# A fused RWKV-5 and SwiGLU kernel: first chunk loaded by halves, one table on another engine, merged stores, branch hints and a new order of all operations

## Chip, cores and metric

The kernel runs on one core of a Trainium2 chip. The metric is the device time of one execution in microseconds (us). Each time given as a median comes from several executions; a profiled execution is one more, taken with the hardware profiler, whose span runs from the first to the last instruction.

## What is computed

Two blocks follow each other. The first is a linear attention with a decaying state: for each of 4 batches and 8 heads, a 48 x 48 state runs over 768 time steps. The second takes its output as 3072 tokens of 384 features, normalises each by its root mean square and applies a gated feed-forward layer with 1536 hidden features.

```python
for t in range(S):                                   # S = 768, D = 48
    cur = einsum('bhd,bhe->bhde', u * k[t], v[t])
    y[t] = einsum('bhd,bhde->bhe', r[t], state + cur)
    state = w * state + einsum('bhd,bhe->bhde', k[t], v[t])
x = y.transpose(0, 2, 1, 3).reshape(B * S, H * D)    # (3072, 384)
xn = x / sqrt(mean(x * x) + 1e-6) * rms_g
g = xn @ w_gate
out = (g * sigmoid(g) * (xn @ w_val)) @ w_out
```

All inputs are float32; the weights arrive as float64 and are cut to 32 bits on the chip.

## The kernel before

**Tiling.** The 768 steps are cut into 12 chunks of 64 (`NS`, `L`). For a chunk, the attention is turned into matrix products: scores of r against k with powers of w folded in, masked, times v; plus r against the state. With 4 batches a chunk gives 256 tokens for the feed-forward layer. The 8 heads lie as 2 x 4 on the two halves of 64 partitions. Chunks 0 and 1 go through the layer as plain products while the weights still arrive; from chunk 2 on, chunks go in pairs, with a scheme that needs seven products for eight.

**Mixing of chunk 0** (`mixing`, L807, with `quick`). It works on two halves of the batches, q = 0 and 1, so that one half can go ahead. `CH` holds r and k of a chunk, channels on partitions. ScalarE makes ku = k times u (`u_k`, L466), four products a half. VectorE makes `RR` = r times the table `up`; VectorE (half 0) and GpSimd (half 1) make k times the table `down` in place (`decay`, L440). TensorE makes the products E of ku and r and A of k and RR (`products`, L482), 32 matmuls a half. VectorE takes the diagonal from E and the rest from A into the masked scores `MT`. TensorE makes the outputs Y = `MT` times `V` (`first_outputs`, L516). ScalarE then keeps them (yT), their squares (sq) and a copy with the partition halves exchanged (yb, L629). The squares give the norm: TensorE sums them, GpSimd takes a power, VectorE refines it and puts it on a diagonal (diag), a matmul spreads it to all rows (spread) and ScalarE copies it. Chunk 0's first hidden products start before the norm is there, and take it in afterwards.

**Tables.** `powers` (L327) raises w to the powers 0 to 63 on VectorE into `pw`. `up` is `pw` over w to the 32nd, made by `table_up` (L339) with eight ScalarE products of 64 columns; `down` is the mirror image, one VectorE product of 512 columns.

**Weights.** SP loads them in pieces of 384 or 576 numbers a partition (`piece`, L395) into six raw buffers. ScalarE (ulp) and VectorE (two operations on bits) cut each piece, and GpSimd adds the two parts. At most four loads are in flight (`IN_FLIGHT`): the fifth is issued when the first has landed (`at_most`, L164).

**Order.** Every operation is first added to a plan with an engine, a cost and the keys that it reads and writes. `Plan.give` (L230) then issues all operations in the order of the list `ORDER` (L83), written out as numbers: each engine runs its own operations in that order. Waits follow from data alone. Before the first useful matmul, `warm` (L1095) issues some matmuls of 512 columns on a tile of ones, as many as the planned start of that matmul leaves room for.

**End.** The fast path holds for a range of inputs only. It counts violations into `bad`; behind the last matmul each engine loads that number (`load`, L1289), and `program` (L1698) branches over a general version of some 5,000 instructions when it is zero. In the program text the general version comes directly behind the fast one, so with zero every engine jumps. The last results leave by `result` (L1171): with 64 rows to a DMA, the two halves of the rows go out on SP and ScalarE, and the very last piece by two DMAs on ScalarE.

**Stores of chunks 0 and 1.** `store` (L674) issues a DMA for each 64 rows, four a chunk.

Of the kernel before, what the change touches and what calls it, by code (L numbers as in the profile page):

```python
# [61 lines left out]
HP = H // 2  # L62
# [10 lines left out]
def feature_order():  # L73
# [10 lines left out]
    0, 4, 5, 14, 9, 6, 1, 39, 19, 3, 8, 2, 16, 17, 24, 11, 44, 12, 40, 41, 29, 43, 45, 10, 42, 47, 74, 99, 46, 49, 50,  # L84
    20, 13, 56, 48, 15, 51, 96, 57, 18, 34, 25, 7, 52, 58, 26, 27, 53, 21, 60, 22, 63, 59, 31, 109, 64, 23, 54, 65,
    55, 81, 66, 104, 61, 62, 28, 67, 114, 30, 82, 68, 119, 32, 69, 122, 70, 75, 101, 33, 83, 76, 86, 102, 100, 87, 36,
    77, 120, 106, 78, 35, 71, 121, 98, 80, 123, 97, 79, 37, 130, 124, 107, 196, 73, 191, 125, 38, 91, 105, 201, 127,
    72, 103, 126, 92, 129, 128, 108, 115, 88, 131, 110, 116, 145, 132, 151, 117, 188, 133, 111, 152, 112, 193, 270,
    153, 113, 93, 134, 135, 187, 275, 136, 118, 206, 197, 190, 137, 155, 138, 156, 194, 139, 159, 157, 192, 140, 198,
    280, 141, 199, 160, 142, 195, 285, 154, 161, 148, 200, 144, 162, 189, 163, 143, 203, 146, 214, 164, 147, 211, 171,  # L90
    165, 158, 89, 94, 212, 172, 213, 167, 173, 202, 150, 174, 168, 208, 237, 183, 169, 204, 271, 170, 223, 302, 205,
    184, 166, 179, 185, 209, 207, 215, 276, 307, 180, 268, 186, 210, 175, 149, 181, 218, 272, 176, 224, 277, 278, 217,
    251, 182, 177, 282, 220, 273, 216, 274, 221, 219, 247, 84, 222, 252, 178, 95, 248, 253, 281, 254, 348, 243, 249,
    286, 283, 225, 90, 322, 279, 250, 267, 312, 317, 226, 349, 244, 238, 229, 259, 287, 245, 85, 227, 263, 246, 304,
    230, 260, 303, 228, 305, 288, 261, 231, 284, 262, 327, 232, 255, 350, 332, 289, 264, 233, 256, 306, 265, 257, 240,
    351, 357, 269, 294, 266, 319, 314, 295, 309, 374, 298, 296, 239, 258, 297, 299, 313, 315, 290, 300, 358, 301, 310,
    291, 308, 234, 318, 337, 387, 311, 241, 408, 292, 361, 391, 360, 352, 323, 392, 316, 293, 236, 242, 354, 388, 320,
    321, 389, 353, 355, 359, 407, 342, 356, 329, 324, 334, 330, 390, 362, 325, 561, 326, 363, 399, 333, 335, 235, 565,
    338, 564, 328, 400, 364, 366, 367, 393, 331, 365, 573, 562, 368, 339, 343, 369, 563, 340, 336, 370, 571, 341, 344,
    394, 570, 371, 381, 410, 372, 375, 384, 345, 376, 382, 383, 405, 346, 377, 373, 378, 409, 439, 347, 568, 587, 395,  # L100
    440, 379, 594, 574, 406, 396, 567, 397, 566, 572, 401, 418, 398, 593, 411, 385, 569, 402, 620, 412, 413, 414, 403,
    575, 621, 404, 622, 576, 441, 577, 447, 442, 579, 444, 448, 588, 449, 415, 443, 445, 589, 630, 450, 446, 580, 380,
    453, 451, 452, 454, 581, 458, 624, 455, 457, 460, 459, 582, 462, 461, 623, 463, 456, 632, 590, 464, 629, 465, 595,
    466, 592, 591, 469, 467, 419, 468, 416, 646, 472, 417, 470, 421, 477, 473, 471, 578, 653, 583, 479, 478, 474, 420,
    386, 625, 424, 652, 485, 476, 480, 481, 486, 631, 627, 487, 482, 475, 626, 633, 496, 483, 484, 488, 797, 491, 489,
    584, 497, 498, 422, 492, 628, 493, 504, 423, 495, 499, 427, 500, 505, 425, 506, 798, 490, 501, 585, 494, 502, 634,
    503, 635, 800, 507, 510, 508, 509, 515, 511, 513, 512, 517, 516, 514, 638, 426, 523, 639, 430, 518, 519, 524, 636,
    525, 799, 520, 428, 534, 647, 521, 522, 648, 526, 801, 804, 529, 527, 535, 530, 640, 536, 531, 810, 533, 528, 542,
    537, 586, 532, 539, 429, 543, 433, 431, 538, 540, 641, 545, 541, 544, 553, 548, 554, 432, 649, 546, 549, 809, 436,
    599, 637, 651, 550, 547, 650, 555, 551, 600, 552, 596, 601, 802, 806, 603, 556, 434, 597, 558, 598, 437, 607, 435,  # L110
    606, 438, 807, 604, 803, 605, 602, 608, 829, 642, 654, 557, 805, 611, 560, 823, 559, 830, 643, 655, 644, 610, 645,
    609, 612, 808, 656, 613, 811, 615, 614, 860, 616, 812, 617, 856, 813, 815, 816, 659, 817, 618, 683, 657, 619, 658,
    685, 684, 824, 691, 686, 857, 662, 688, 692, 818, 693, 687, 689, 694, 690, 858, 825, 697, 695, 702, 698, 859, 699,
    704, 703, 696, 701, 710, 660, 705, 661, 700, 707, 711, 665, 663, 814, 868, 708, 826, 706, 713, 709, 712, 716, 714,
    721, 717, 718, 720, 723, 722, 715, 729, 664, 724, 719, 666, 726, 730, 667, 725, 727, 869, 671, 668, 862, 731, 732,
    728, 866, 882, 735, 733, 740, 736, 737, 739, 742, 741, 734, 748, 865, 743, 738, 863, 745, 749, 744, 746, 751, 747,
    669, 750, 754, 752, 753, 759, 755, 670, 756, 674, 761, 760, 758, 831, 889, 763, 762, 757, 764, 827, 767, 765, 766,
    770, 768, 769, 773, 771, 772, 778, 774, 828, 775, 672, 780, 819, 779, 675, 861, 673, 777, 781, 888, 786, 676, 677,
    867, 680, 776, 783, 787, 788, 782, 784, 789, 785, 864, 792, 790, 791, 793, 870, 795, 794, 796, 832, 835, 820, 834,
    872, 836, 838, 871, 873, 681, 874, 837, 875, 678, 833, 679, 876, 1036, 839, 877, 1033, 878, 682, 843, 879, 821,  # L120
    1034, 840, 881, 822, 880, 846, 844, 883, 1035, 842, 1039, 1043, 1037, 1042, 847, 891, 884, 845, 1040, 892, 848,
    885, 849, 1059, 921, 850, 851, 919, 894, 852, 887, 920, 853, 886, 893, 895, 922, 841, 854, 1038, 855, 924, 927,
    925, 1041, 923, 928, 898, 1044, 1066, 890, 930, 926, 929, 933, 931, 938, 934, 935, 937, 940, 939, 896, 897, 946,
    941, 1045, 901, 943, 947, 932, 948, 936, 942, 899, 944, 1046, 957, 945, 900, 949, 904, 952, 950, 1092, 958, 959,
    951, 953, 954, 965, 956, 960, 902, 1047, 1093, 903, 955, 907, 1065, 1048, 962, 966, 961, 963, 1060, 967, 1049,
    968, 964, 971, 969, 1051, 976, 1094, 972, 978, 977, 973, 970, 975, 984, 979, 905, 1052, 980, 985, 1098, 986, 974,
    981, 1101, 995, 982, 983, 987, 990, 988, 996, 997, 991, 992, 906, 994, 1053, 998, 999, 989, 910, 1054, 993, 1000,
    1003, 1001, 1002, 1006, 1004, 1095, 908, 1061, 1009, 1005, 1096, 909, 1014, 1102, 1010, 1007, 1011, 1062, 1015,
    1067, 1118, 1018, 1099, 1013, 1125, 911, 1016, 1064, 913, 912, 1022, 1017, 1008, 916, 1105, 1063, 1019, 1023,
    1104, 1012, 1020, 1097, 1021, 1124, 1025, 1100, 1050, 1103, 1028, 1026, 1027, 1029, 1106, 1024, 1030, 1031, 1032,  # L130
    1071, 1068, 914, 1055, 917, 915, 1072, 1069, 1074, 918, 1056, 1070, 1058, 1107, 1079, 1269, 1073, 1108, 1075,
    1080, 1110, 1111, 1272, 1273, 1112, 1076, 1078, 1083, 1113, 1077, 1109, 1270, 1271, 1119, 1114, 1082, 1084, 1115,
    1116, 1085, 1120, 1121, 1081, 1117, 1087, 1155, 1127, 1088, 1156, 1089, 1123, 1057, 1122, 1282, 1128, 1281, 1295,
    1276, 1129, 1302, 1279, 1274, 1090, 1157, 1130, 1091, 1126, 1086, 1163, 1158, 1160, 1164, 1278, 1165, 1159, 1161,
    1275, 1166, 1162, 1174, 1167, 1131, 1134, 1168, 1169, 1175, 1176, 1170, 1171, 1173, 1182, 1177, 1277, 1178, 1183,
    1184, 1172, 1179, 1193, 1180, 1181, 1185, 1280, 1188, 1186, 1328, 1187, 1283, 1194, 1189, 1190, 1132, 1192, 1195,
    1133, 1285, 1137, 1201, 1196, 1191, 1198, 1202, 1135, 1203, 1296, 1197, 1199, 1136, 1212, 1200, 1297, 1140, 1329,
    1301, 1284, 1204, 1207, 1205, 1213, 1214, 1208, 1206, 1209, 1211, 1220, 1138, 1215, 1330, 1216, 1221, 1139, 1222,
    1210, 1217, 1335, 1143, 1334, 1231, 1218, 1287, 1141, 1223, 1142, 1288, 1219, 1146, 1224, 1289, 1226, 1332, 1225,
    1232, 1233, 1227, 1331, 1228, 1239, 1230, 1234, 1235, 1240, 1341, 1229, 1290, 1236, 1241, 1250, 1237, 1238, 1242,  # L140
# [40 lines left out]
class Plan:  # L181
# [30 lines left out]
    def times(self, order, free):  # L212
# [3 lines left out]
        for i in order:  # L216
# [9 lines left out]
            if locks:  # L226
                port[e] = end[i]
        return start

    def give(self, order, free, idle, final):  # L230

        assert sorted(order) == list(range(len(self.ops)))
        start, busy = self.times(order, free), 0.0
        last = next(i for i in reversed(order) if self.ops[i][0] == "PE")
        for i in order:
# [4 lines left out]
            if i == last:  # L240
                final()
# [1541 lines left out]
```

## Time and profile before

| | us |
|---|---|
| median of 3 executions | 603.48 |
| lowest, highest | 599.68, 604.60 |
| the profiled execution | 599.91 |
| its span, first to last instruction | 598.2 |

| engine | busy us of the span | share |
|---|---|---|
| TensorE matmul (PE) | 583.4 | 98% |
| TensorE weight load (PEld) | 512.6 | 86% |
| VectorE (DVE) | 411.2 | 69% |
| ScalarE (ACT) | 296.2 | 50% |
| GpSimd (POOL) | 46.2 | 8% |

How to read the profile: almost all lines carry L178, since one helper issues every operation; groups are told apart by the tiles, written out<-in. Waits are put down to the semaphore that came last. The page cuts the span into 40 slices and gives each engine's busy share in tenths, so that a hole in an engine's work can be placed; the DMA row does the same for the 16 DMA engines. Times of branches and semaphore instructions are shown but not counted as busy. A matmul's end is modelled, so a busy PE does not mean that it runs at its peak.

### The profile page before, as it was taken

To read this page: it belongs to the slowest core of one execution; us is meant where nothing else is said; L and a number is where in the kernel's file an instruction comes from. 1 tells how busy PE (TensorE), PEld (TensorE's weight loads), DVE (VectorE), ACT (ScalarE), POOL (GpSimd) and SP (SyncE) were. 2 spreads that over 40 slices of the span, in tenths; PEclk is the share of its full clock that TensorE was granted. 3 is DMA by queue.
4 is the path that set the end of the run, shared out by engine and by line. 5 is a ranking of instruction groups with operands and counts; after the bars stand their busy time and mean duration, and the time that the engine had idled before them with its cause. 6 is when DMAs were issued, how large, how long until landed. Compare 5 with 4: busy or idle time off the path is not lost.

```text
span 598.2 us, 16446 instructions
## 1 busy us (share of the span) xinstructions
PE 583.4 (98%) x7202; PEld 512.6 (86%) x7202; DVE 411.2 (69%) x621; ACT 296.2 (50%) x721; POOL 46.2 (8%) x40
## 2 busy tenths in 40 slices
PE   7889999999999999999999999999999999999995
PEld 4678888667888899888899888899888899988995
DVE  7857786877887786666877566878558775455631
ACT  6755666663656633662383356627355652113300
POOL 3342323600000000000000000000000000000000
PEclk8989999999999999999999999999999999999999
DMA  8786384125251233213302530501523200201001
GB/s 283 262 280 256 133 291 141 53 69 173 67 201 32 62 119 116 65 54 115 125 8 67 168 113 28 211 10 35 169 65 115 95 9 1 80 28 54 2 22 38
DMA packets 22546, 62.99 MB, mean 105 GB/s; under 512 B 2977, under 2 KB 9793, under 8 KB 21057
## 3 DMA queue, kind: packets, MB, share of 16 engines
q1 hardware_dynamic: 21760, 61.41, 30.5%
q8 instruction: 58, 0.95, 0.7%
q10 hardware_dynamic: 704, 0.44, 0.3%
q14 instruction: 24, 0.19, 0.1%
HBM read 56.04 MB, written 4.72 MB: 102 GB/s over the span
## 4 chain that ended last, share of the span: by engine, by line
PE 94%; DVE 2%; ACT 1%; issue 1%; DMA 1%; POOL 0%; SPq 0%; DVEq 0%; ACTq 0%
PE bank_b L178 32%; PE bank_a L178 26%; PE bank_c L178 26%; PE at L178 10%; DMA chan<-in_chan_dram 1%; DVE RR L178 1%; DVE bits L178 0%; ACT ku L178 0%; DVE MT L178 0%; ACT up L178 0%; DVE ms L178 0%; ACT ST L178 0%; DVE KH L178 0%; POOL ms L178 0%; SPq L178 0%
## 5 line engine op out<-in xcount | busy, mean ns | idle before, releaser
L178 DVE TENSOR_TENSOR gv<-bank_b,m 128x512 f32<-128x512 f32 x90 | 62.1, 690 | 60.6 <-PE bank_b L178 59.0
L178 ACT ACTIVATE gv<-gv 128x512 f32<-128x512 f32 (+1 forms) x60 | 31.2, 524 | 72.5 <-DVE gv L178 71.8
L178 DVE TENSOR_TENSOR gv<-bank_c,gv 128x512 f32<-128x512 f32 x60 | 41.5, 691 | 23.6 <-PE bank_c L178 23.2
L178 PE MATMUL bank_b<-xa,wa 64*128 64x256 f32 x444 | 55.8, 385 | 0.0
L178 PEld LDWEIGHTS bank_b<-xa,wa 64*128 64x128 f32 x444 | 43.4, 191 | 5.6 <-issue 0.3
L178 PE MATMUL bank_a<-xa,wa 64*128 64x256 f32 x372 | 45.6, 378 | 0.0
L178 PE MATMUL bank_a<-xb,wb 64*128 64x256 f32 x372 | 45.6, 378 | 0.0
L178 PE MATMUL bank_a<-wo,h 128*128 128x192 f32 x264 | 45.6, 329 | 0.0
L178 PE MATMUL bank_b<-t,s 64*128 64x256 f32 x360 | 44.5, 379 | 0.0
L178 PE MATMUL bank_c<-t,s 64*128 64x256 f32 x360 | 44.2, 378 | 0.0
L178 PE MATMUL bank_b<-t,wb 64*128 64x256 f32 x360 | 44.1, 377 | 0.0
L178 PE MATMUL bank_c<-xb,s 64*128 64x256 f32 x360 | 44.0, 377 | 0.0
L178 PEld LDWEIGHTS bank_a<-wo,h 128*128 128x128 f32 x264 | 42.9, 190 | 0.5
L178 ACT COPY m<-bank_a 128x512 f32<-128x512 f32 (+1 forms) x35 | 19.9, 570 | 46.9 <-PE bank_a L178 31.7
L178 ACT ACTIVATE MT<-dmask,du 128x64 f32<-128x64 f32 x160 | 41.3, 339 | 1.3 <-DVE du L178 1.2
L178 PEld LDWEIGHTS bank_a<-xb,wb 64*128 64x128 f32 x372 | 35.8, 187 | 4.6 <-issue 0.6
L178 PEld LDWEIGHTS bank_a<-xa,wa 64*128 64x128 f32 x372 | 35.8, 187 | 4.6 <-issue 0.6
L178 ACT ACTIVATE rows_out<-rows_out 128x384 f32<-128x384 f32 x72 | 39.2, 558 | 0.4
L178 DVE TENSOR_TENSOR h<-gv 128x256 f32<-128x256 f32 (+1 forms) x60 | 32.6, 551 | 9.2 <-ACT gv L178 9.0
L178 PEld LDWEIGHTS bank_c<-xb,s 64*128 64x128 f32 x360 | 34.8, 187 | 4.3 <-issue 0.3
L178 PEld LDWEIGHTS bank_c<-t,s 64*128 64x128 f32 x360 | 34.6, 187 | 4.3 <-DVE h L178 0.3
L178 PEld LDWEIGHTS bank_b<-t,wb 64*128 64x128 f32 x360 | 34.7, 187 | 4.0
(179 smaller groups left out, 1074.5 us busy)
## 6 DMA issues: line engine op xcount, KB each, us to landing
chan<-in_chan_dram SPq DMA_DIRECT2D x11, 1024.0 KB, 6.9
TOK<-in_tok_dram SPq DMA_DIRECT2D x10, 768.0 KB, 5.5
V<-in_vpad_dram SPq DMA_DIRECT2D x12, 512.0 KB, 4.6
raw<-in_wot_dram SPq DMA_DIRECT2D x8, 576.0 KB, 4.3
rows_out<-in_wka_dram SPq DMA_DIRECT2D x12, 384.0 KB, 3.3
rows_out<-in_wkb_dram SPq DMA_DIRECT2D x12, 384.0 KB, 3.3
rows_out<-in_wot_dram SPq DMA_DIRECT2D x12, 384.0 KB, 3.2
out_dram<-rows_out SPq DMA_DIRECT2D x41, 96.0 KB, 2.8
```

The source lines that it names most:

```text
L178: return lambda *args, **kwargs: self.tc.keep_in_program_order(give(*args, **kwargs))
```

## The change

The change has six parts.

- `loads(0)` issues r and k of chunk 0 as four DMAs, one for each half of the batches, instead of two. A half has 2 KB a partition.
- `table_up` is one VectorE product of 512 columns, with the factors repeated by the access pattern.
- `store` sends the results of a chunk with two DMAs, each with two batches of 64 rows, instead of four.
- `result` sends the last piece by one DMA on SP and one on ScalarE.
- Ahead of the fourth matmul group from the end, each engine gets a branch hint for the branch over the general version, behind its last instruction issued by then; the branch is marked to prefer falling through.
- `ORDER` is another permutation. The formula for the number of warm-up matmuls has other constants; three are issued instead of four.

In the new order SP's queue begins: the small columns, r half 0, k half 0, k half 1, r half 1, one weight piece, V, four weight pieces, r and k of chunk 1, k by tokens of chunk 1, six large or small weight pieces, V of chunk 1. Before, it began: the columns, k, two weight pieces, r, a weight piece, V, two weight pieces, a large one, r and k of chunk 1, a weight piece, k by tokens, three large pieces, V of chunk 1.

```diff
 ORDER = [
-    0, 4, 5, 14, 9, 6, 1, 39, 19, 3, 8, 2, 16, 17, 24, 11, 44, 12, 40, 41, 29, 43, 45, 10, 42, 47, 74, 99, 46, 49, 50,
+    0, 4, 7, 5, 6, 8, 1, 11, 41, 10, 2, 16, 3, 42, 43, 21, 45, 26, 12, 46, 44, 76, 47, 49, 31, 48, 51, 52, 17, 13, 53,
...
-    def give(self, order, free, idle, final):
+    def give(self, order, free, idle, hint, final):
...
-        last = next(i for i in reversed(order) if self.ops[i][0] == "PE")
+        last = [i for i in order if self.ops[i][0] == "PE"][-4:]
         for i in order:
+            if i == last[0]:
+                hint()
...
-            if i == last:
+            if i == last[-1]:
                 final()
...
     def table_up():
-        for x in range(2 * HP):
-            act.mul(flat3(up)[:, x], pw[:, x], winv[:, x : x + 1])
+        dve.tensor_mul(flat3(up), pw, by_inv)
...
-    def store(osb, s, j):
+    def store(sums, s):
         for bl in range(2):
-            row = (2 * j + bl) * S + s * L
-            sp.dma_start(out=out[row : row + L, :], in_=osb[bl * L : (bl + 1) * L, :])
+            to = bass.AP(
+                tensor=out.tensor, offset=out.offset + (bl * S + s * L) * DM, ap=[[DM, L], [2 * S * DM, 2], [1, DM]]
+            )
+            sp.dma_start(out=to, in_=sums[bl * L : (bl + 1) * L])
...
             for i, x in ((1, "k"), (0, "r")):
-                add(
-                    "SP", 1.5, [], [f"CH{x}0", f"CH{x}1"],
-                    lambda i=i: sp.at_most(IN_FLIGHT, lambda: sp.dma_start(out=CH[:, i], in_=chan[s, :, i])), land=LAND, name=f"load {x} {s}",
-                )
+                for q in range(2):
+                    half = slice(2 * q, 2 * q + 2)
+                    add(
+                        "SP", 0.75, [], [f"CH{x}{q}"],
+                        lambda i=i, half=half: sp.at_most(
+                            IN_FLIGHT, lambda: sp.dma_start(out=CH[:, i, half], in_=chan[s, :, i, half])
+                        ), land=LAND, name=f"load {x} {s}",
+                    )
...
-    add("ACT", 2.0, ["pw", "h3.1", "h3.2"], ["up"], table_up, name="up")
+    add("DVE", 0.65, ["pw", "h3.1", "h3.2"], ["up"], table_up, port=True, name="up")
...
-            for _ in range(int((until - 4.5) / 0.9)):
+            for _ in range(int((until + 0.4 - 3.75) / 0.86)):
...
-            if last and k == 1 and js == (1,):
-                add("ACT", 1.0, keys, [f"stored {s} {k} {js}'"], lambda: give((0, 1), act), land=2.5, name="store")
-            elif last:
+            if last:
                 add("SP", 0.6, keys, [f"stored {s} {k} {js}"], lambda: give((0,), sp), land=2.5, name="store")
                 add("ACT", 0.6, keys, [f"stored {s} {k} {js}'"], lambda: give((1,), act), land=2.5, name="store")
...
+    def hint():
+        traced = nc.cur_bb.bb.instructions
+        for engine in mybir.ALL_ENGINES:
+            with tc.issue_after(next(i for i in reversed(traced) if i.engine == engine)):
+                tc.mark_branch_hint_location("general", "LikelyTaken", [engine])
...
-    with tc.If(n_bad > 0):
+    with tc.If(n_bad > 0, preferred_fallthrough_block=True, label="general"):
```

## The prediction

> **What bounds the kernel now.** I read first the busy time by stage, since a mean over the span hides where TensorE idles. Columns: stretch in us, its length, then busy us of PE, weight loads, VectorE, ScalarE and GpSimd, granted clock, DMA share, GB/s.
>
> ```profile
> core 0: us, PE busy (x) PEld busy (x) DVE busy (x) ACT busy (x) POOL busy (x), PEclk, DMA share, GB/s
> 0.00:9.50 9.50, 6.23 (x8) 2.37 (x8) 5.43 (x24) 5.58 (x18) 1.42 (x11) 1.00 0.77 259
> 9.50:18.00 8.50, 7.40 (x237) 6.78 (x237) 6.97 (x16) 5.92 (x18) 4.91 (x4) 0.80 0.87 305
> ...
> 38.00:591.50 553.50, 553.50 (x6563) 490.30 (x6560) 380.06 (x550) 271.05 (x657) 30.94 (x19) 1.00 0.28 94
> 591.50:598.20 6.70, 0.01 (x1) 0.00 (x0) 0.36 (x1) 0.00 (x0) 0.00 (x0) 0.89 0.12 33
> ```
>
> From 38 us to 591.5 us PE never pauses, and the change takes no matmul from it. So time can be won only in the first 38 us and in the last 6.7 us, and lost anywhere. The 6.23 us of PE work before 9.5 us are 8 warm-up passes that compute nothing. Next the chain of waits for the head: start, us, what.
>
> ```profile
> 1.25 4.06 DMA chan<-in_chan_dram
> ...
> 5.40 1.28 ACT ku L178 x4
> 6.68 1.91 ACT up L178 x8
> 8.59 0.89 ACT ku L178 x3
> ...
> 9.52 2.37 DVE RR L178 x2
> ...
> 14.28 1.05 PE bank_c L178 x32
> 15.34 0.86 issue
> ...
> 35.10 1.73 issue
> ```
>
> k of chunk 0 lands at 5.31; ScalarE then makes half of ku, all of up, then the other half of ku, and VectorE's RR starts at 9.52, because r, issued fourth, lands at 9.42. The two pieces "issue" are stalls for which the profile names no data. Last the instructions of the branch line, for the tail:
>
> ```profile
> L1704 PEldq COMPARE_BRANCH  x1: 3912/3912/3912, 589.0 to 589.0; - x1
> L1704 SPq COMPARE_BRANCH  x1: 45/45/45, 590.5 to 590.5; - x1
> L1704 ACTq COMPARE_BRANCH  x1: 54/54/54, 593.3 to 593.3; - x1
> L1704 ACTq EVENT_SEMAPHORE  x1: 17/17/17, 597.0 to 597.0; - x1
> ```
>
> ScalarE branches at 593.3 and its next instruction runs at 597.0: 3.7 us for a jump. SP branches at 590.5 and runs on at 594.0: 3.5 us.
>
> [...]the two RR products took 0.69 and 1.76 us, the second beside GpSimd's 1.49. [...]four in flight share some 350 GB/s, and 512 KB took 4.06 us.
>
> **The change, part by part.**
>
> *Loads.* Before, SP issues k, two weight pieces, r. After: r half 0, k half 0, k half 1, r half 1, then one weight piece, V. That is two issues more (2 x 0.43 us on SP, hidden: SP waits for landings anyway). Behind them the first weight piece is issued when the first half lands instead of at 1.7 us; VectorE takes it later (below). The second half to be issued completes 512 KB, as k alone did, so I take 5.3 for k half 0; 5.9 and 6.4 for the next two at 350 GB/s. Bounds: [...]6.3 (before, the second transfer landed at 6.25).
>
> *Table up.* Removed: 8 ScalarE products, 2.0 us. Added: one VectorE product, 0.69 us by the row of its twin "down", which took 4.70 to 5.39. VectorE is idle 0.88 us there, waiting for weights; cover enough. It ends at 5.4, down at 6.1.
>
> *The head, step by step.* ScalarE: ku 5.4 to 6.65 and 6.65 to 7.95 (1.28 each). VectorE: RR half 0 6.1 to 6.8, k half 0 to 7.5, RR half 1 to 8.2 (0.69 each). GpSimd: k half 1 8.0 to 9.5 (1.49). PE: scores E at 6.7 and 8.0, A half 0 to 9.2 (0.57 for 32 matmuls, half of the 1.15 at half clock). VectorE: mask 9.3 to 10.05 (0.77). PE: outputs half 0 10.1 to 11.0 (0.9), where before they ran 13.30 to 14.2: 3.2 us earlier. VectorE now puts one weight piece (0.36 + 0.56) between the halves, so its last mask ends at 12.45 against 14.56: 2.1 earlier. But ScalarE, which comes next, is loaded first by half 0: yT 0.89, squares 0.5, a copy 0.5, a weight piece 0.55, squares, yT, three copies: 11.1 to 16.5, against 20.05 before. 3.5 earlier. The norm, then the spread matmul, start at 18.1, against 21.69.
>
> *What is late next.* Chunk 1's r and k (1 MB) can only be issued when A half 1 has read chunk 0's: 11.6 against 13.31. Before it took 6.87 us, so 18.5; by bytes alone 16.3. ScalarE's order puts ku of chunk 1 (1.28) and a weight piece (0.55) ahead of the copy of the norm, so that copy comes at 18.7 to 20.4, against 22.42. So 2.0 to 3.7 us of the lead survive. The weights do not eat it: in the trace wa and wb of the second quarter are ready at 32.15 and 33.52 and used at 37.98 and 40.56.
>
> *The clock and the two stalls.* With three warm-up rows for four (4.7 us of work for 6.23) [...]one window at half clock may fall on the outputs of chunk 0: 0.9 + 0.57 us more, at worst 1.5 lost. The 0.86 stall may vanish, as the stretch before it is now spread out: between 0 and 0.86 won. The 1.73 at 35.1 sits in a run of 64-row products that the new order keeps as dense: I take no change, 0 to 1.73 won[...]. I take 3.0 us for the whole head, 0.5 to 6.
>
> *The order after 38 us.* PE changes its kind of product (full, halves, quarters) 93 times instead of 90; a change costs 0.1 to 0.2 us (groups of 1.50 against 1.29 hold one or two). 0.3 us lost. Whether new waits arise the trace can't show; bounds 0 and, by the rival below, some us.
>
> *Merged stores of chunks 0 and 1.* Two SP issues for four, twice: 4 x 0.33 to 0.4 us off a queue that nobody waits for then; the landings hide behind PE. Nothing.
>
> *Tail.* The last result was stored by two ScalarE DMAs one after the other, 591.94 and 592.45, the second 0.81 us long and 3.9 us to landing: 596.3. From there to the end 1.85 us (SP's row of waits, two barriers). After: one on SP, one on ScalarE, both at 592.0. The stores around took 1.9 to 4.1 us to landing, median 2.7; I take 2.1[...]: 594.1, and the end at 595.95. 2.2 us won. That needs the hint: without it SP jumps at 592.45 + 3.5 and the end is at 597.9: 0.3 won. The hint is not in the trace[...]. The five hint instructions themselves should cost no more than the branch, 45 ns. I take the hint as working; the general path still lies first in the program, so the jump remains.
>
> Sum: 3.0 - 0.3 + 2.2 = 4.9 us. The profiled execution took 599.91 (span 598.2 and 1.7 around it); after: 595.0. It lies 3.6 us below the median of the runs shown, 603.48; the same difference there gives 598.6.
>
> **Rivals.** (1) *More*: [...]4.9 + 0.86 + 1.73 + 1.0 = 8.5 us, 595.0. For it: both stalls lie where DMA is 0.87 and 0.77 busy; against: the same instructions, as dense. (2) *The hint does nothing*: 4.9 - 1.9 = 3.0, 600.5. For it: no row shows one. (3) *The head wins nothing*, because four halves share the DMA engines and land together at 8 us (before, the third transfer landed at 8.15): tail alone, 601.5. (4) *Slower: V of chunk 1.* On SP it stands behind six weight pieces that follow the 1 MB load and the small token load (before, four), 8.85 MB into the stream instead of 8.26. Its outputs stood at 33.57 on PE, with no other work before them. By 13.5 us 3.54 MB had landed; at 350 GB/s from there V lands at 28.7, in time; the point is 38.6, 5 us after the old place (head lead and tail gain used up), a stream of 211 GB/s from 13.5 us on. Before it ran 253 at 20 to 30 us. Each us beyond is a us lost; a DMA queue that waits for raw buffers could bring 44.8: 603.48 + 6.2 = 609.7.
>
> **How the numbers follow.** 1% (6.03 us) is about what a measurement of this kernel can tell from no change. Forecast 0.57: 598.6, own range 596.5 to 600.5; a quarter of it is over 1% faster. Rival 1: 0.19, faster. Rival 2: 0.11 and rival 3: 0.05, within 1%. Rival 4: 0.08, nearly all slower. Faster 0.14 + 0.19 = 0.33; slower 0.07; the same 0.60. The range 594.5 to 604.5 leaves out half of rival 4 and the ends of rival 1 and of the forecast's.
>
> **What would show it.** In the profile after: k half 0 landing by 5.9, RR starting near 6.1, outputs of chunk 0 near 10, the spread near 18 to 20, PE without a pause from 36 on; in the tail under 0.6 us between each branch and the next instruction, and the last store's landing about 2 us after its issue. I am wrong if PE shows gaps after 38 us, if the branch still costs 3.5 us, or if the outputs of chunk 1 start after 32.

## The result, and the profile after

The changed kernel takes 599.02 us (median of 20 runs, 596.73 to 602.77) where the kernel before, run beside it, takes 599.98 (20 runs): a ratio of 0.9992 with a 95% interval of 0.9968 to 1.0015. No change that this measurement can tell from none. The prediction said 4.9 us less; by the ratio about 0.5 came (0.96 between the medians), and the interval reaches from 1.9 us less to 0.9 more. The profiled execution took 598.84 us, span 597.1, against 599.91 and 598.2 before. The rest of the document looks for the missing 4 us.

First the busy time by stage of the changed kernel, with the stretches of the table shown of before. Columns: stretch, length, then busy us of PE, weight loads, VectorE, ScalarE and GpSimd, granted clock (the share of its full clock that TensorE was given), DMA share, GB/s.

```profile
core 0: us, PE busy (x) PEld busy (x) DVE busy (x) ACT busy (x) POOL busy (x), PEclk, DMA share, GB/s
9.50:18.00 8.50, 6.87 (x140) 6.33 (x140) 4.53 (x13) 5.67 (x16) 2.31 (x3) 0.58 0.92 322
18.00:23.40 5.40, 4.99 (x27) 3.60 (x26) 4.48 (x10) 2.95 (x9) 2.87 (x3) 0.72 0.95 342
23.40:38.00 14.60, 12.06 (x359) 9.88 (x363) 13.71 (x21) 9.57 (x20) 5.79 (x5) 1.00 0.80 277
38.00:591.30 553.30, 553.09 (x6589) 489.61 (x6577) 388.69 (x554) 270.80 (x657) 29.04 (x19) 1.00 0.29 94
```

From 38 us on TensorE pauses for 0.21 us in all, in one new wait at 107.5 us. What is new is the clock: 0.58 in 9.5 to 18 us where before it was 0.80, and 0.72 in the next stretch. The clock records show half clock from 10.83 to 21.07 us, 10.24 us in a row; before, it lay at 9.69 to 13.10 and at 36.99 to 40.41, 3.41 and 3.42 us long. So a window means here a stretch of 3.41 us at half clock: the changed kernel has three in a row. Now the chain of waits of the head: start, us, what.

```profile
6.28 1.22 PE bank_c L178 x32
...
9.29 0.77 DVE MT L178 x2
...
10.36 1.20 PE at L178 x48
...
15.43 2.65 PE at L178 x12
18.08 4.28 PE bank_a L178 x24
22.36 0.64 PE at L178 x2
...
23.03 0.37 ACT diag L178
...
36.31 1.32 issue
37.63 0.77 PE at L178 x37
```

The front works as planned: E starts at 6.28, and the outputs of chunk 0 ("at", x48) at 10.36, where they started at 13.30. But the copy of the norm ("ACT diag") comes at 23.03, where before it came at 22.42. A lead of 2.9 us has become a lag of 0.6, and the chain names TensorE itself for it: mean squares 2.65 us, the first 24 weight products 4.28. The products are not alone in their place. While TensorE made them, the norm went its own way over GpSimd and VectorE, and its diagonal was ready (22.23) just when TensorE was free to spread it (22.29):

```profile
21.75 0.48 DVE L178 TENSOR_SCALAR diag<-ident,ms 128x128 f32<-128x128 f32 x2
...
22.29 0.70 PE L178 MATMUL at<-diag,ones 128*128 128x256 f32 x2
```

In the other runs of the new head without fillers the spread came 0.35 to 1.2 us behind the diagonal, so there the products at half clock did hold it up. Last the branch line, for the tail.

```profile
L1715 PEldq COMPARE_BRANCH  x1: 398/398/398, 589.2 to 589.2; - x1
L1715 DVEq COMPARE_BRANCH  x1: 84/84/84, 591.4 to 591.4; - x1
L1715 SPq COMPARE_BRANCH  x1: 70/70/70, 592.3 to 592.3; - x1
L1715 ACTq COMPARE_BRANCH  x1: 73/73/73, 593.2 to 593.2; - x1
L1715 DVEq EVENT_SEMAPHORE  x1: 21/21/21, 594.3 to 594.3; - x1
L1715 ACTq EVENT_SEMAPHORE  x1: 17/17/17, 595.9 to 595.9; - x1
```

TensorE's branch takes 0.40 us instead of 3.91. VectorE still jumps from 591.4 to 594.3 and ScalarE from 593.2 to 595.9; SP goes on at 595.2, 2.9 us after its branch. The hint reached one engine of five (GpSimd's jump, from 565.7 to 568.5 us, is hidden behind other work), and not one that the end waits for. From the start of VectorE's last addition to the end of the span it takes 5.73 us, before 6.62: 0.9 won.

### The profile page after: what moved, and what is told of

It is laid out like the page before. It is cut to its first block, busy times and chain, and to the rows that moved or that the text cites. A ratio compares the mean times of both kernels' runs of the same rounds, so it can differ in the third digit from the quotient of the medians.

```text
span 597.1 us, 16433 instructions
## 1 busy us (share of the span) xinstructions
PE 584.2 (98%) x7200; PEld 513.2 (86%) x7200; DVE 418.3 (70%) x622; ACT 294.2 (49%) x713; POOL 42.6 (7%) x40
## 4 chain that ended last, share of the span: by engine, by line
PE 96%; ACT 1%; DMA 1%; issue 1%; DVE 1%; SPq 0%; ACTq 0%; DVEq 0%
PE bank_b L178 32%; PE bank_a L178 27%; PE bank_c L178 26%; PE at L178 11%; DMA chan<-in_chan_dram 1%; ACT ST L178 0%; ACT ku L178 0%; DVE KH L178 0%; DVE MT L178 0%; ACT yT L178 0%; ACT wk L178 0%; SPq L178 0%; ACT ulp L178 0%; ACT diag L178 0%; ACT last_heads L178 0%
## 5 line engine op out<-in xcount | busy, mean ns | idle before, releaser
L178 ACT ACTIVATE gv<-gv 128x256 f32<-128x256 f32 (+1 forms) x60 | 30.9, 522 | 70.7 <-DVE gv L178 70.5
L178 PEld LDWEIGHTS bank_b<-xa,wa 64*128 64x128 f32 x444 | 42.1, 187 | 6.1 <-DVE TOK L178 0.7
L178 ACT ACTIVATE gv<-bank_a 128x256 f32<-128x256 f32 x30 | 11.5, 383 | 54.6 <-PE bank_a L178 54.6
L178 PEld LDWEIGHTS bank_b<-t,s 64*128 64x128 f32 x360 | 34.5, 187 | 4.3 <-issue 0.3
```

The lines of the kernel that those rows point to most:

```text
L178: return lambda *args, **kwargs: self.tc.keep_in_program_order(give(*args, **kwargs))
```

## The experiments

All were timed in five rounds beside the kernel before, in three sessions, in which the kernel before took 600.86 us (fillers, no hint, early hints on VectorE and SP, split store only), 599.84 (after again, all together, whole loads, before + fillers) and 600.31 (the other four). Ratios are those to the kernel before in the same session; they are not quotients of the medians and differ from these by up to 0.002.

Each timing comes with its mean granted clock. In 209 timings of the kernel before, time = 595.3 + 0.74 x (span x (1 - clock)), correlation 0.90. So the clock of TensorE, which no part of the change aims at, goes with most of the spread of 594 to 605 us. Where "at equal clock loss" is said below, all timings were fitted together with one slope (0.70 us for each us lost) and one constant for each kernel; the residual is 1.06 us, and the changed kernel (42 timings) stands at 1.09 +- 0.36 us below the kernel before. This figure is an estimate with limits. It counts lost clock in the tail, where TensorE is idle (from 594.51 us in the changed kernel's profile), and the slope within a single kernel goes from 0.05 (table on ScalarE) to 1.24 (before + fillers). By it the fillers would stand 0.6 us above the kernel before and the kernel without warm-up 3.2 us above, which their medians don't show. It is of use between kernels that lose about as much clock.

| kernel | median us | ratio to before | 95% interval |
|---|---|---|---|
| after, first comparison | 599.02 | 0.9992 | 0.9968 to 1.0015 |
| after again | 598.87 | 0.9991 | 0.9975 to 1.0008 |
| after + fillers | 597.37 | 0.9960 | 0.9939 to 0.9982 |
| after, no hint | 598.45 | 0.9957 | 0.9936 to 0.9977 |
| after, early hints (VectorE, SP) | 598.20 | 0.9971 | 0.9954 to 0.9988 |
| after, early hints on all | 597.85 | 0.9976 | 0.9954 to 0.9997 |
| after + fillers + early hints on all | 596.73 | 0.9959 | 0.9940 to 0.9978 |
| after, whole loads | 599.64 | 0.9991 | 0.9971 to 1.0010 |
| after, table on ScalarE | 600.07 | 1.0010 | 0.9989 to 1.0030 |
| after, no warm-up | 599.32 | 1.0001 | 0.9976 to 1.0026 |
| before, split store only | 599.28 | 0.9995 | 0.9971 to 1.0018 |
| before, split store + early hints | 598.11 | 0.9957 | 0.9934 to 0.9980 |
| before + fillers | 599.22 | 0.9995 | 0.9966 to 1.0024 |

### Fillers in the pauses of the head

```diff
+    FILL = {0: 2, 1: 1, 2: 1, 3: 3, 5: 1, 6: 1}
     def warm(since, until):
+        if since == until:
+            for _ in range(FILL.get(since, 0)):
+                pe.matmul(bank_of["a"][:, 1, 384:512], ones, ones, start=True, stop=True, skip_group_check=True)
```

(The key counts the matmul groups; the columns are used by nothing else there.)

> The changed kernel with nine filler matmuls of 128 columns that compute nothing, put where TensorE stood still before 14 us (two before E half 0, one before E half 1, one before A half 0, three before Y half 0, one before Y half 1, one before the mean squares); about 0.39 us each at full clock by the warm-up rows. Clock theory: the lead of 2.9 us at Y half 0 was lost because TensorE dropped to half clock from 10.8 to 21.1 us after a stretch with idle gaps of 0.89 and 1.21 us. Then the granted clock of 9.5 to 18 us is 0.9 or more (0.58 in the changed kernel), the spread matmul comes at 20.0 or earlier (22.29), and the time falls by 1 to 2.5 us to 596.5 to 598.0. Load theory: chunk 1's r and k land at 19.25 anyway and ScalarE's order holds the rest, so the clock is full but the first even stretch of TensorE starts no earlier than 38 us and the time stays at 598.5 to 599.5. If gaps are not what sets the clock, it stays near 0.6 and the time is 599.0 to 600.

Measured: clock 1.000 in the profiled run, and over the 22 timings a mean loss of 2.4 us to the clock, against 6.8 and 6.1 for the changed kernel in its two comparisons. The stages of this run, and its chain:

```profile
9.50:18.00 8.50, 6.61 (x165) 5.81 (x165) 5.64 (x15) 6.74 (x18) 3.96 (x4) 1.00 0.93 326
18.00:23.40 5.40, 3.69 (x30) 2.30 (x31) 5.23 (x11) 4.01 (x15) 1.85 (x3) 1.00 0.92 361
```

```profile
10.59 0.91 PE at L178 x48
...
14.64 1.25 PE at L178 x12
...
16.22 0.96 POOL ms L178
...
18.19 0.93 DVE ms L178
...
19.54 0.49 DVE diag L178 x2
...
20.08 0.71 PE at L178 x2
...
20.82 0.37 ACT diag L178
...
34.12 1.28 issue
35.40 1.00 PE at L178 x55
```

The same 48 outputs take 0.91 us instead of 1.20, the mean squares 1.25 instead of 2.65, and the copy of the norm comes at 20.82 instead of 23.03, although the outputs began 0.2 us later. The last matmul ends at 589.34 instead of 591.34. So 2.0 us came back with the clock in these profiled runs, and 1.5 to 1.7 by the medians. The median is within the theory's range and outside the rivals'. But not all of the lead came back: it is 2.7 us at the outputs and 1.6 at the copy of the norm (20.82 against 22.42 before). The chain also shows what bounds the head once TensorE is fast: the norm's path over GpSimd and VectorE, 4.2 us from the end of the mean squares (15.88) to the spread matmul (20.08). The spread missed the expected 20.0 by 0.08. In the kernel before, the same path from the mean squares (18.08) to the ready diagonal (21.21) took 3.1 us:

```profile
18.42 0.72 POOL ms L178
...
19.16 0.95 DVE ms L178
...
20.14 0.17 DVE ms L178
...
20.93 0.28 DVE diag L178
```

The second VectorE step takes 0.93 us now and took 0.17. Beside the norm GpSimd adds two weight pieces (from 17.14 and 18.10, 1.0 us each); before, one stood there (from 19.09). In all ten profiled runs of the new head the path takes 4.1 to 4.2 us, in all four of the old head 3.1 to 3.2, whatever the clock: the new order made it 1.0 us longer. That the second addition is the cause fits these rows: before, the step beside the one addition took 0.95 us and the step beside none 0.17. It was not tried.

### The same fillers in the kernel before

The key 0 got five and the key 4, ahead of the outputs, three.

> The kernel before with eight filler matmuls of 128 columns that compute nothing: five in TensorE's pause from 7.38 to 9.56 us ahead of E, three ahead of the outputs of chunk 0. Head, order, loads and tail as before. Theory: the half-clock windows of the head are a cost that both kernels pay, and are worth more than the change itself. In 75 timings of the kernel before, time = 595.7 + 0.68 x (us lost to the clock), 7.2 lost in the mean; with the 2.4 that the changed kernel with fillers loses, 597.3. So 597.0 to 598.0, mean clock over 0.993, outputs of chunk 0 still near 13.1 us. Rival, VectorE's chain sets the head and TensorE's clock there is worth nothing: 600 to 601. Rival, only the changed kernel can use the full clock: 598.5 to 600.

A miss: the median fell by 0.6 us, within the noise, and the timings spread over 10 us. The profiled run shows what stood in the way: the three ahead of the outputs fell into a half-clock window and ran from 14.09 to 15.67, while the mask was ready at 14.23. The mask itself was 1.0 us later than before, behind a longer RR. Its chain:

```profile
9.70 3.20 DVE RR L178 x2
...
13.03 2.71 PE bank_a L178 x38
15.74 1.53 PE at L178 x48
```

The outputs began at 15.74 instead of 13.30. So this run does not say what the kernel before would do at full clock; that stays open. It shows that a filler ahead of critical work has a price, here 1.4 us.

### No warm-up

`for _ in range(0)` in place of the three warm-up matmuls.

> The changed kernel without its three warm-up matmuls (they compute nothing). Theory: the clock of the head costs about 0.7 us for each us lost to it; without warm-up TensorE does all of the head up to 18 us or later at half clock, the mean loss rises from 6.4 us (42 timings) to 8 or more, and the time by 1.2 to 2.5 us, to 600 to 601.3. Rival, clock of the head is worth nothing because VectorE, ScalarE and loads set the chain: 598.4 to 599.4.

The rival's number came, 599.32, and half of the reason is a trap in the records. The page gives this run a clock of 0.999. But its matmuls run at the slow rate to 23 us (chain of waits):

```profile
10.44 1.56 PE at L178 x48
...
15.31 2.65 PE at L178 x12
17.95 5.32 PE bank_a L178 x24
```

At full clock the 48 outputs took 0.91 us and the mean squares 1.25 (fillers). Yet the profile lists a clock of 1.00 for every stage of this run up to 38 us, so here slow time is counted as full; why was not shown. The rest of the reason: a head wholly at half clock ends its last matmul at 592.22, only 0.9 us later than the changed kernel's 591.34 with three slow windows, while the full clock gives 589.34. The changed kernel is already near its bad end. So of the 2.9 us between the two ends the changed kernel pays 2.0 already; the theory's 1.2 to 2.5 us more were not there to be lost.

### The parts of the head undone

Loads whole (r first, then k; `WITH` is 0 for both, so the second of each pair issues nothing):

```diff
-                            IN_FLIGHT, lambda: sp.dma_start(out=CH[:, i, half], in_=chan[s, :, i, half])
-                        ), land=LAND, name=f"load {x} {s}",
+                            IN_FLIGHT, lambda: sp.dma_start(out=CH[:, i], in_=chan[s, :, i])
+                        ) if q == WITH[x] else None, land=LAND, name=f"load {x} {s}",
```

> The changed kernel with chunk 0's r and k loaded whole (r first, then k, 512 KB each) where it loads four halves; table on VectorE, order, stores and hint as changed. Theory: r lands near 5.0, k near 7.2, the outputs of chunk 0 start at 12 to 12.7 (10.36 with halves), and as the lead of the halves is spent at half clock anyway, the time is within 0.7 us of the changed kernel. Rival, the prediction's view that a us at the outputs is nearly a us at the end: 1.3 to 2 us slower. It could even be faster by 0.5 to 1 us if the later, denser work keeps the full clock.

The outputs began at 11.67 instead of 10.00 (the changed kernel beside it). The ratio is the same, 0.9991 and 0.9991, but the median is 0.8 us higher (599.64 against 598.87), between the theory's 0.7 and the rival's 1.3 to 2. In the profiled runs the lead of the halves lasts: with whole loads the copy of the norm comes at 24.54 instead of 22.95, and the last matmul ends at 592.79 instead of 591.39. With one profiled execution each and timings that spread over 5 us, what the halves are worth at the end stays open. The mean clock loss is larger, 7.4 against 6.1 us.

Table up on ScalarE (the `act.mul` loop of before, "ACT" for "DVE" in `add`):

> The changed kernel with table up made by ScalarE's eight products again, between its two halves of ku (as before); loads by halves, order, stores and hint as changed. Theory: E half 1 comes after 9.5 us (7.45), the outputs of chunk 0 start near 11.5 to 12.5 (10.0 to 10.4), and the 1.5 to 2 us are worth little at the end, since TensorE at half clock is what carries the chain from there to the spread matmul: 598.5 to 599.8, at equal clock loss within 0.6 us of the changed kernel. Rival, the prediction's: 1.3 to 2 us slower, 600.2 to 601.

The outputs began at 11.89, the copy of the norm came at 25.84 instead of 23.03, and the last matmul ended at 592.66 instead of 591.34. The median is 600.07, above the theory's range and just under the rival's 600.2 to 601, and 1.1 us above the changed kernel's two medians, which are of other sessions; the ratio is 0.002 above the changed kernel's, and the intervals overlap. At equal clock loss it is no slower (1.02 +- 0.48 below before, against 1.09), but in this kernel's timings clock and time hardly go together. So the table is likely worth about 1 us at the end; whether it is paid by way of the clock (loss 7.9 us) was not shown.

### The tail

The tail is counted here from the start of VectorE's last addition; the expectations with 5.37 or 6.27 us in them count from its end, 0.36 us later.

Hint left out (`lambda: None` in place of `hint`):

> The changed kernel without the branch hints, all else kept. Theory: the hint reached TensorE alone, whose branch is off the path that sets the end; so TensorE's branch costs 3.9 us again, VectorE's, ScalarE's and SP's cost 2.7 to 3.6 as before, from the end of VectorE's last addition to the end of the span still 5.2 to 5.6 us (5.37), and the time stays at 598.5 to 599.5. Rival, the hint earns the tail's gain: from the last addition to the end 6.0 us or more and the time 599.7 to 601. Rival, the hint costs: 0.3 to 0.5 us less than the changed kernel.

TensorE's branch took 4.07 us again, the other three as with the hint. In the profiled run the last store landed at 596.71, where with the hint it landed at 594.76, and the tail was 6.82 us, as the rival had it. But the timings do not follow the profile: 598.45, and at equal clock loss 0.88 +- 0.48 below before, which is the changed kernel's 1.09 within the error. One profiled tail of 6.8 us is not a mean. Its ratio, 0.9957, is as low as that of the fillers in the same session: single ratios here can't be ranked. That the changed hint is worth nothing measurable is what the timings say.

Split of the last store alone, in the kernel before:

> The kernel before with only the last store split over SP and ScalarE as in the changed one; no hint, head and order as before. Theory: the split alone earned the tail's 0.9 us: from the last addition to the end 5.3 to 5.5 us (6.27 before, 5.37 after), time 599.0 (before 599.98). Rival, as the prediction had it, SP's jump of 3.5 us then ends last and only 0.3 us is won: 5.9 to 6.1 us, time 599.7. If it brings nothing: 600.0.

Nothing: 0.9995, tail 6.81 us. SP's branch stands at 590.5 and its first wait behind the branch at 594.5.

```profile
L1702 SPq EVENT_SEMAPHORE  x8: 17/17/17, 594.5 to 595.0; - x8
...
L1702 SPq COMPARE_BRANCH  x1: 45/45/45, 590.5 to 590.5; - x1
L1702 ACTq COMPARE_BRANCH  x1: 54/54/54, 590.5 to 590.5; - x1
...
L1702 ACTq EVENT_SEMAPHORE  x1: 17/17/17, 594.2 to 594.2; - x1
```

Both stores had landed at 593.96, before SP could ask for them. The jump ends last, as the prediction had said of the case without a hint; but not even its 0.3 us came.

Hints earlier: on VectorE, SP and ScalarE the hint is tied to an instruction further back.

```diff
+    EARLIER = {nc.scalar.engine: 66, nc.vector.engine: 66, nc.sync.engine: 66}
...
-            with tc.issue_after(next(i for i in reversed(traced) if i.engine == engine)):
+            of = [i for i in traced if i.engine == engine]
+            with tc.issue_after(of[-min(EARLIER.get(engine, 1), len(of))]):
```

> The changed kernel with the hints of ScalarE, VectorE and SP put 97, 94 and 118 instructions ahead of their branches, where in the changed kernel they stand 9, 10 and 8 ahead. Theory: [...]the three branches cost under 0.6 us each, the last store's landing (2.4 us after its issue) sets the end, from the last addition to the end 4.5 us (5.37), and the time is 598.0 to 598.4. Rival, these engines ignore hints: branches of 2.7 to 2.9 us, 598.7 to 599.3.[...]

VectorE's jump fell to 0.61 us and SP's to 0.52. ScalarE's stayed at 2.71. The tail is 4.76 us. A half hit: two engines follow the theory, the third does not. Then ScalarE's hint was moved to 146 instructions ahead, with 110 in place of 66:

> The changed kernel with the early hints of ScalarE, VectorE and SP (146, 94 and 118 instructions ahead), no fillers: the tail alone. Theory: jumps under 0.7 us on all three, from the last addition to the end 4.5 to 4.9 us (5.73 and 5.83 in the changed kernel), 0.9 to 1.1 us faster at equal clock loss: 597.5 to 598.2. Rival, the gain with fillers came from the clock alone: 598.7 to 599.2.

The branch line of this run:

```profile
L1718 DVEq COMPARE_BRANCH  x1: 84/84/84, 589.6 to 589.6; - x1
L1718 DVEq EVENT_SEMAPHORE  x1: 21/21/21, 590.2 to 590.2; - x1
L1718 SPq COMPARE_BRANCH  x1: 70/70/70, 590.5 to 590.5; - x1
L1718 ACTq COMPARE_BRANCH  x1: 73/73/73, 591.4 to 591.4; - x1
L1718 ACTq EVENT_SEMAPHORE  x1: 17/17/17, 591.9 to 591.9; - x1
```

All three go on within 0.5 to 0.6 us, and the last store's landing (593.01) sets the end: tail 4.93 us. At equal clock loss 1.77 +- 0.48 below before, 0.7 better than the changed kernel (+- 0.5); the early hints of VectorE and SP alone gave 1.96 +- 0.48, and their tail, with ScalarE's jump still at 2.71 us, was no longer. So there ScalarE's jump was not what the end waited for. By what means a hint acts, and why ScalarE's did nothing at 97 instructions (2.71 us), was not shown.

The same tail on the kernel before (split store and early hints, head and order untouched):

> The kernel before with the tail alone: last store split over SP and ScalarE, and hints 147, 97 and 116 instructions ahead of the branches of ScalarE, VectorE and SP; loads, table, order and merged stores as before. Theory: the split alone brought nothing (6.81 us from the last addition to the end) because SP's and ScalarE's jumps of 3.7 to 4.0 us ended last; with hints that are in time the jumps take under 0.7, from the last addition to the end 4.5 to 5 us, 1.6 to 2.0 us won at equal clock loss: 598.0 to 598.8 where the kernel before shows 599.8 to 600.6. Rival: the hint's 1 us depends on the changed order; under 0.5 us won.

598.11, ratio 0.9957, tail 4.74 us. By ratio this is as good as anything with the new head. At equal clock loss it stands at 0.94 +- 0.48 below before, less than the expected 1.6 to 2.0. In the profiled run SP's jump still took 1.9 us, although its hint stood 116 instructions ahead.

### All together, and the changed kernel again

> The changed kernel as it is, on the same chip as the three beside it. In its own comparison it was 599.02 against 599.98. If the change wins about 1 us, 0.9975 to 0.9995 of the kernel before; if the 4.9 us of the prediction are hidden by a chip, 0.992 or less; if it wins nothing, 1.000.

> The changed kernel with the nine fillers and with the early hints of VectorE and SP, and ScalarE's hint moved further ahead (146 instructions before its branch; at 97 its jump still took 2.71 us). Theory: [...]all three jumps take under 0.7 us, from the last addition to the end 4.4 to 4.8 us (5.6 with fillers alone), and the time is 597.4 - 0.9 = 596.5 (596.1 to 596.9). Rival, ScalarE ignores hints: 2.7 us again, ending at the same time as the last store's landing, 596.3 to 596.9. If the tail is worth nothing in the timed runs: 597.4.

The repeat gave 0.9991, "about 1 us" at most. With fillers and hints in time on all engines, on the same chip, 596.73: 2.1 us faster than the changed kernel by the medians (598.87), and 0.9959 of before. All three jumps took 0.50 to 0.62 us, the tail 4.82. This is the version that beats both; of the kernels here it also has the lowest median. In its profiled run two windows, from 14.94 to 21.77 us, were still at half clock, and the copy of the norm came at 22.30: the fillers make half clock rarer (mean loss 2.2 us, against 6.1) and don't rule it out.

## Why the prediction was right, and where its sum was not

"The same" was right and the time, 598.6, is near the 599.0 measured. That the times agree is luck: the median shown for before, 603.48, came from three executions, and beside the changed kernel it was 599.98, so a start 3.5 us too high made up for most of a gain that was 4.4 us too large. Taken as a difference, 4.9 us were predicted and about 0.5 came. Of the prediction's own signs of being wrong, one came plainly, the outputs of chunk 1 after 32 us (34.73), and two in part, a gap after 38 us (0.21) and branches that still cost 2.7 to 2.9 us. Step by step:

- *Loads.* k half 0 landed at 5.74, the others at 6.45 and 7.09: the first under the bound of 6.3, all three 0.4 to 0.7 us later than taken. The first half, r, landed at 3.85, 2.60 us after its issue.
- *Table.* VectorE's product took 0.69 us at 4.69. As predicted.
- *Front.* Outputs at 10.36 and 10.00 (predicted 10.1). The lead of 3.2 us was there: 2.9 and 3.3. But the wait was another than the predicted one, the mask. The repeat's chain names V, which in the new order stands behind the four halves and a weight piece:

```profile
5.14 4.72 DMA V<-in_vpad_dram
9.87 0.14 issue
10.00 0.91 PE at L178 x48
```

In seven of the eight profiled runs of the new head with halves and the table on VectorE the outputs began 0.13 to 0.14 us after V had landed, with the mask ready 0.3 to 1.3 us before them; in the kernel before V had landed 1.7 us ahead. The prediction gave V's landing no time, so that the number came is luck too. A V issued earlier was not tried.

- *Clock.* "At worst 1.5 lost": this is the step that failed most. It let one window fall on the outputs alone. Three fell in a row, on the outputs, the mean squares and the 24 weight products that stand ahead of the spread in TensorE's order. These I had not counted as path at all, since before VectorE ended last there. At half clock the mean squares are on the path (2.65 us against 1.25 at full clock), and the products (4.28 us) end with the norm's own path or behind it; at full clock the spread is free at 20.08. I had the copy of the norm at 18.7 to 20.4; it came at 23.03, and at full clock at 20.82. That a window might fall on the outputs was my estimate. In the kernel before, half clock from 9.69 stood behind a pause of 2.18 us (7.38 to 9.56), but the busy share of TensorE in the 3.41 us ahead did not decide it alone: 2.20 of 3.41 us (7.42 to 10.83) was followed by half clock, 1.75 of 3.41 in the run with fillers (17.79 to 21.20) was not. With fillers in the pauses the mean loss was 2.4 us, without them 6.8 and 6.1; what sets half clock stays open.
- *Norm.* I let the spread follow ScalarE's last copy by 1.6 us, at 18.1. Even at full clock it came at 20.08, and the copy of the norm 0.4 us after the latest predicted: there the norm's own path of 4.2 us ends last, 1.0 us longer than before and not priced at all.
- *Chunk 1's load* landed at 19.25 (16.3 to 18.5 predicted). The first half of ku of chunk 1 waited 0.39 us for it (19.27), the second ran at 23.29, behind the copy of the norm; the copy waited for TensorE and not for them. The slower rival, V of chunk 1, did not come: V landed at 32.86, and its outputs stood at 34.73, behind other work of TensorE.
- *Stalls.* 0.86 became 0.19, and 1.41 in the repeat; 1.73 became 1.32 and 1.47, and was 0.10 with early hints on all, where nothing in the head was changed. They belong to the single execution. "No change taken" was a fair choice. A third one, 0.16 before, was 0.47 at 31.08.
- *Order after 38 us.* -0.3 was predicted. From the restart behind the second stall to the last matmul, at full clock, the changed order took 553.70 to 553.72 us in five profiled runs (the changed kernel twice, without hint, with early hints, with whole loads), the order of before 553.06 (split store). So -0.65, of which 0.21 is one new wait of TensorE at 107.5 us. In the kernel before the same stretch took 554.68, since a half-clock window lay in it: against that execution the changed kernel gained 1.6 us of clock there, 1.0 after the order's loss, and this hid the lag of 0.8 with which it came out of the head.
- *Tail.* 2.2 predicted, 0.9 in the profile. The landing was near (594.76 for 594.1). The hint was taken as working; it worked on TensorE alone. With hints in time, on VectorE and SP or on all, the tail fell by 1.7 to 1.9 us (6.62 to 4.93, 4.82, 4.76, 4.74): there the predicted gain came nearly in full. The trace of before holds no hint, so the distance at which one works could not be read from it.
- *Merged stores*, costed at nothing, were not tried alone.

For the head alone the runs leave this. Its parts give a real lead of 3 us at the outputs. Behind the second stall, where 3.0 us were to be won, the profiled changed kernel was 0.8 late. The clock takes about half of these 3.8 us; that was shown by giving it back, which brought 2.0 in the profile. The rest did not come back with it. At full clock (fillers) TensorE's first twelve products behind the second stall began at 36.33; in the run with the old head and the split store they began at 37.17, behind nearly the same stall (1.28 and 1.33), although two windows of that head, from 9.79 to 16.62, were at half clock. They cost the old head nothing at the copy of the norm: 22.44, with one window 22.42. So the new head at full clock leads by 0.8 us, and the new order takes 0.65 of it back before the last matmul. What is missing from 3 us there is about the outputs' wait for V (0.9), the longer norm's path (1.0) and a stall of 0.85 us for 0.18: an estimate from single executions, and none of the three was tried. The old head at full clock was not measured, as the fillers in the kernel before failed.

## What to carry to other kernels

A lead at the start of a chain is worth only what the next joins leave of it, so price there every wait, also those that were hidden before: TensorE's work at half clock, when a change moves small matmuls apart (mean squares 2.65 us, 1.25 at full clock); the steps that get new neighbours on VectorE and GpSimd (0.93 us, before 0.17); and each transfer that the new order moves back. A branch hint had to stand well ahead of its branch here: 94 to 118 instructions did on VectorE and SP (jumps of 0.5 to 0.7 us), but once not on SP (1.9), and 146 and 147 on ScalarE (0.5 to 0.6); at 8 to 10 the jumps of these three took 2.7 to 2.9 us in the changed kernel, as without a hint. So look at every engine's gap behind its branch, and at the one on which the end waits. And compare timings at equal granted clock where their spread is larger than the effect.

## What was not expected of the hardware

- The time of one and the same kernel spreads over 10 us, and most of it goes with the granted clock: 209 timings of the kernel before, 594.4 to 605.06, 0.74 us for each us of clock lost, correlation 0.90.
- The profile's mean clock can count slow time as full: the run without warm-up, with 48 outputs in 1.56 us (0.91 at full clock), mean squares in 2.65 (1.25) and its matmuls slow up to 23 us, is listed at 0.999.
- A jump of SP, VectorE or ScalarE took 2.7 to 2.9 us in the changed kernel, whose hints stand 8 to 10 instructions ahead, 2.8 to 2.9 with the hint left out of it, and 0.5 to 0.6 with the early hints on all three.
- Two VectorE steps of the norm, on 128 x 2 numbers each, took 0.95 and 0.17 us before and 0.96 and 0.93 in the new order, where a GpSimd addition runs beside each; before, one ran beside the first alone.
- In the run with the table on ScalarE, whose hint stood as in the changed kernel, ScalarE's jump took 1.06 us, in the changed kernel 2.7. So the distance of the hint alone did not set these times; what else did stays open.
